# Attention and two feed-forward layers on one core: the last phase's weights brought to float32 during phase 1, their sums and splits spread over two steps, the gating product moved from GpSimd to VectorE

## The chip, the cores and the metric

The kernel runs on one core of a Trainium2 chip. The metric is device microseconds (us) of one execution; the median of the executions shown counts, and lower is better. Engines are called PE (TensorE, matrix multiply; PEld are its weight loads), DVE (VectorE), ACT (ScalarE), POOL (GpSimd) and SP (SyncE, which here only issues DMAs).

## The reference, cut to what matters

```python
x = attn(q, k, v, mem_k, mem_v)          # 3072 tokens x 512, chunked attention with 8 memory keys
h = x @ w_in                             # 512 -> 2048
x1 = softplus(h) @ w_out                 # 2048 -> 512
a, b = x1 @ w_a, x1 @ w_b                # 512 -> 1536 each
out = (a * b) @ w_o2                     # 1536 -> 512, float32
```

Inputs come as 64-bit floats, so every weight tile of 128 x 512 values (512 KB) is first brought to float32 by integer operations, and then split into a rounded high part and a low part; each product of two float32 matrices is made of three matmuls (high by high, high by low, low by high).

## The kernel before

The 3072 tokens are 8 tiles of 384. **Phase 1** runs, for each tile t and each of 16 f-steps, 12 matmuls of `emit_h` (L450), softplus and a split in `emit_soft` (L456 to L460, L437, L440), and, two f-steps later, 12 matmuls of `emit_x1` (L473), which accumulate x1; x1 goes to a scratch in DRAM (L481, L482). In tiles 0 to 6 the attention of later tokens is woven in by a list `plan` of (slot, step): tile t, f-step f stands at slots 2*(16*t+f) and the one after. In tile 0 the 32 tiles of w_in and w_out are converted and stay in SBUF, in the pool `wp` of 33 buffers with tag "w".

**The last phase** works on pairs of tiles (4 pairs p) in 12 steps f (`pair_step`). Of 2 x 2 blocks of x1 and of the weights w_a and w_b, sums are formed so that 7 products of 6 matmuls each (L623) do the work of 8 (a Strassen-Winograd scheme). The products run in the order X(11), Y(s2), W(s3), V(s1), X(12), W(22), V(s4); behind Y the DVE adds q = Y + s (L675), behind W r = W + q (L686), behind V d22 (L693); the second W product adds to the bank that r was read from, so it waits for r. c2 = d21 * d22 is formed on POOL (L703), rounded on ACT (L705), and its low part is formed on POOL (L706); c1 is formed on DVE (L714, ACT L716, DVE L717, the last one put off to the next step behind q). Between products, `next_job` runs parts of the output product (`job`, L646, six matmuls, then an addition on DVE, L655), six jobs for every two steps.

The weights of the last phase go through `Conversion`, one for each f: three fetches of 512 KB (w_a, w_b, w_o2; L548), an ACT operation on each (`top`, L532), two DVE operations on each (`val`, L534 and L535), four subtractions of 256 columns on POOL (`sums`, L566 to L569), the high parts on ACT (L579, L587), the low parts on POOL (L583) and DVE (L591), and five stores to scratches for pairs 1 to 3 (L598, L599). Conversions 0 to 2 run in tile 7 of phase 1, conversions 3 to 11 in pair 0, each within one step, three steps ahead of its use: `at(k)` is called seven times in a step, and runs the next entry of `steps()`. The sums and splits of x1 for pair 0 (`pieces`, L500 to L522) run on DVE in f-steps 10 to 15 of tile 7.

In tile 0, tile 7 and the last phase, the order of every engine's queue is the order of the program text; in tiles 1 to 6 that holds for PE and DVE alone, and a scheduler orders SP, ACT and POOL.

Of the kernel before, what the change touches and what calls it, by code (L numbers as in the profile page):

```python
# [9 lines left out]
F32 = mybir.dt.float32  # L10
# [7 lines left out]
TT = 384  # L18
# [18 lines left out]
LAST_CV = ((0, 4), (3, 7), (6, 10))  # L37
LAST_X1 = (7, 10)
PAIR_CV = 3
# [4 lines left out]
def attn_moe_moe2(ctx: ExitStack, tc: tile.TileContext, q, k, v, mem_k, mem_v,  # L44
# [28 lines left out]
    ud = nc.dram_tensor("u_scratch", (NF2, 4, P, 1024), F32, kind="Internal").ap()  # L73
    w2od = nc.dram_tensor("w2o_scratch", (NF2, P, 1024), F32, kind="Internal").ap()
# [413 lines left out]
    PLACE = {"11": (0, 0), "12": (0, 1), "s2": (1, 0), "s3": (1, 1), "s1": (2, 0), "22": (2, 1), "s4": (3, 0)}  # L488
# [35 lines left out]
    cv, us, w2o = {}, {}, {}  # L524

    def bits(val, raw, half):

        words = raw.rearrange("p (n two) -> p two n", two=2)
        low, high = words[:, 0], words[:, 1]
        if half == 0:  # L530
            top = high.bitcast(F32)
            nc.scalar.activation(top, top, AF.Prelu, scale=2.0 ** -112, alpha=-(2.0 ** 32))  # L532
        else:
            nc.vector.tensor_scalar(val, low, 29, None, ALU.logical_shift_right)  # L534
            nc.vector.scalar_tensor_tensor(val, high, 3, val, ALU.logical_shift_left, ALU.bitwise_or)  # L535

    class Conversion:


        def __init__(self, f):  # L540
            self.f = f
            self.raw = {}

        def fetch(self, n):
            f = self.f
            src = w_o2[f * P:(f + 1) * P, :] if n == "o" else (w_a if n == "a" else w_b)[:, f * P:(f + 1) * P].rearrange("(k p) f -> p k f", p=P)
            raw = self.raw[n] = wp.tile([P, 1024], U32, tag="w", name=f"raw_{n}{f}")
            nc.sync.dma_start(raw if n == "o" else raw.rearrange("p (a b) -> p a b", a=KT), src.bitcast(U32))  # L548

        def top(self, n):  # L550
            bits(None, self.raw[n], 0)

        def val(self, n):
            f = self.f
            if n == "a":
                self.v = wp.tile([P, 2, 512], U32, tag="w", name=f"v{f}")
            if n == "o":
                self.vo = mp.tile([P, 512], U32, tag="tmp", name=f"vo{f}", bufs=2)
            bits(self.vo if n == "o" else self.v[:, n == "b"], self.raw[n], 1)

        def sums(self, engine):
            v = self.v.bitcast(F32).rearrange("p n (k f) -> p n k f", k=2)
            b11, b21, b12, b22 = v[:, 0, 0], v[:, 0, 1], v[:, 1, 0], v[:, 1, 1]
            self.t = t = wp.tile([P, 4, 256], F32, tag="w", name=f"t{self.f}")
            t2, t3, t1, t4 = (t[:, i] for i in range(4))
            engine.tensor_tensor(t1, b12, b11, ALU.subtract)  # L566
            engine.tensor_tensor(t2, b22, t1, ALU.subtract)
            engine.tensor_tensor(t3, b22, b12, ALU.subtract)
            engine.tensor_tensor(t4, b21, t2, ALU.subtract)  # L569
# [94 lines left out]
    def pair_step(p, f, at, between=()):  # L664
# [11 lines left out]
        if late_lo:  # L676
            late_lo.pop()()
# [231 lines left out]
```

## Time and profile before

| what | value |
|---|---|
| median of 3 executions | 1280.59 us (1280.18 to 1280.63) |
| the profiled execution: its own time, its span | 1282.68 us, 1280.6 us |
| busy: PE, PEld, DVE, ACT, POOL | 94%, 88%, 54%, 42%, 30% of the span |
| tiles 1 to 6 of phase 1 | 154.7 to 604.3 us, 75 us each |
| tile 7 | 604.3 to 673.5 us |
| pair 0 | 673.5 to 855.05 us, 181.55 us |
| pairs 1 and 2 | 137.51 us each |
| pair 3 and the end | 1130.08 to 1280.6 us |

A stage ends where the first matmul of the next one starts. PE's matmuls are pipelined: six matmuls of 384 columns start 1.04 us apart as a group and six of 512 columns 1.39 us, so a step of a pair in which PE never waits takes 7 x 1.04 + 3 x 1.39 = 11.46 us; all steps of pairs 1 and 2 take that.

### The profile page before, as it was taken

The numbers are of one execution on the slowest core, as the hardware profiler recorded it, in microseconds if no ns is written. First come the engines' busy times: TensorE is split into PE (matmuls) and PEld (weight loads), VectorE is DVE, ScalarE is ACT, GpSimd is POOL, SyncE is SP. The second block draws the span as 40 slices with busy tenths as digits, with TensorE's granted clock in tenths as the row PEclk, the third lists the DMA queues.
The fourth block names the chain that finished last, engine by engine and source line by source line (L and its number), as shares of the span: only waits on it lengthen the run. The fifth ranks groups of instructions, "written<-read, shape, count | busy, mean of one in ns | idle before, by whom it ended". The sixth has DMA issues, their size and how long they took to land. (4 is left out here: it accounts for less than half of the span.)

```text
span 1280.6 us, 20711 instructions
## 1 busy us (share of the span) xinstructions
PE 1198.8 (94%) x7584; PEld 1124.7 (88%) x7584; DVE 692.4 (54%) x1618; ACT 540.4 (42%) x1333; POOL 383.0 (30%) x357
## 2 busy tenths in 40 slices
PE   5778899999999999999997888799999999999998
PEld 4677899999999999999996777699999999999997
DVE  4785644544444454444487666654445445553554
ACT  4775765565556555555663433222112111122110
POOL 1000023223222322222235776821144112431111
PEclk9997999999999999999998999899999999999999
DMA  8792313213041311300557777439844785549621
GB/s 177 200 292 56 68 37 57 55 30 71 12 75 37 58 48 31 73 14 13 188 215 252 269 251 275 180 129 329 298 170 148 249 342 192 204 150 383 211 87 50
DMA packets 205889, 191.30 MB, mean 149 GB/s; under 512 B 141659, under 2 KB 166363, under 8 KB 205787
## 3 DMA queue, kind: packets, MB, share of 16 engines
q1 hardware_dynamic: 205275, 189.90, 46.9%
q8 instruction: 60, 0.98, 0.3%
q14 instruction: 42, 0.34, 0.1%
q0 software_dynamic: 512, 0.07, 0.0%
HBM read 149.03 MB, written 40.89 MB: 148 GB/s over the span
## 5 line engine op out<-in xcount | busy, mean ns | idle before, releaser
L450 PE MATMUL ph<-x,w 128*128 128x384 f32 x1536 | 298.8, 342 | 12.8 <-ACT x L407 6.2
L450 PEld LDWEIGHTS ph<-x,w 128*128 128x128 f32 x1536 | 272.9, 192 | 18.9 <-ACT x L407 7.3
L646 PE MATMUL py<-w2o,c 128*128 128x512 f32 x864 | 227.3, 398 | 2.9 <-ACT c L705 1.8
L460 DVE SCALAR_TENSOR_TENSOR g<-ph,e 128x384 f32<-128x384 f32 x128 | 71.3, 557 | 266.8 <-ACT e L458 263.1
L646 PEld LDWEIGHTS py<-w2o,c 128*128 128x128 f32 x864 | 162.3, 190 | 31.7 <-POOL c L706 2.9
L705 ACT CAST c<-c 128x384 fp32r<-128x384 f32 x48 | 24.7, 514 | 328.6 <-POOL c L703 325.4
L703 POOL TENSOR_TENSOR c<-d,d 128x384 f32<-128x384 f32 x48 | 50.9, 1059 | 286.2 <-DVE d L701 286.2
L456 ACT ACTIVATE e<-ph 128x384 f32<-128x384 f32 x128 | 62.3, 487 | 136.0 <-PE ph L450 121.2
L623 PE MATMUL pX<-x,u 128*128 128x384 f32 x576 | 116.9, 337 | 2.6 <-ACT s L670 1.6
L655 DVE TENSOR_TENSOR y<-py,y 128x512 f32<-128x512 f32 x120 | 82.8, 690 | 61.7 <-PE py L646 61.7
L623 PEld LDWEIGHTS pX<-x,u 128*128 128x128 f32 x576 | 103.0, 190 | 7.8 <-ACT s L670 2.5
L623 PE MATMUL pW<-xx,u 128*128 128x384 f32 x288 | 63.0, 356 | 21.4 <-DVE r L686 21.4
L375 DVE STREAM_TRANSPOSE af<-sm 32x256 f32<-32x256 f32 x180 | 78.2, 435 | 2.5
L623 PEld LDWEIGHTS pW<-xx,u 128*128 128x128 f32 x288 | 53.7, 200 | 24.3 <-DVE r L686 24.3
L458 ACT ACTIVATE e<-e 128x384 f32<-128x384 f32 x128 | 67.3, 526 | 4.1
L457 ACT ACTIVATE e<-e 128x384 f32<-128x384 f32 x128 | 67.3, 526 | 4.0
L314 ACT ACTIVATE sm<-sm,st 128x96 f32<-128x96 f32 x168 | 60.6, 362 | 6.3 <-DVE st L310 6.3
L701 DVE TENSOR_TENSOR d<-pW,q 128x384 f32<-128x384 f32 x48 | 26.7, 557 | 66.8 <-PE pW L623 66.8
L623 PE MATMUL pV<-xs,u 128*128 128x384 f32 x288 | 58.7, 339 | 3.1 <-DVE xo L481 3.1
L623 PE MATMUL pV<-xx,u 128*128 128x384 f32 x288 | 59.1, 340 | 0.0
L623 PE MATMUL pW<-xs,u 128*128 128x384 f32 x288 | 57.9, 335 | 0.0
L623 PE MATMUL pY<-xs,u 128*128 128x384 f32 x288 | 57.6, 334 | 0.0
(232 smaller groups left out, 2234.7 us busy)
## 6 DMA issues: line engine op xcount, KB each, us to landing
u<-u_scratch SPq DMA_DIRECT2D x108, 512.0 KB
u_scratch<-u SPq DMA_DIRECT2D x36, 512.0 KB
w2o<-w2o_scratch SPq DMA_DIRECT2D x36, 512.0 KB
u<-u_scratch SPq DMA_DIRECT2D x36, 256.0 KB
raw<-in_moe_w_in_dram SPq DMA_DIRECT2D x16, 512.0 KB
raw<-in_moe_w_out_dram SPq DMA_DIRECT2D x16, 512.0 KB
vn<-in_v_dram SPq DMA_DIRECT2D x35, 176.0 KB
raw_a<-in_moe_w_a_dram SPq DMA_DIRECT2D x12, 512.0 KB
```

What stands on the lines that cost most here:

```text
L314: nc.scalar.activation(sm[:, h], sm[:, h], AF.Exp, bias=st[:, 0, h:h + 1], scale=-1.0, accum_out=st[:, 1, h:h + 1])
L375: nc.vector.transpose(out=af[32 * kb:32 * kb + 32, x], in_=self.sm[32 * x:32 * x + 32, :, 32 * kb:32 * kb + 32])
L450: nc.tensor.matmul(ph, lhsT=a, rhs=c, start=n == 0, stop=n == 3 * KT - 1)
L456: nc.scalar.activation(e, ph, AF.Abs)
L457: nc.scalar.activation(e, e, AF.Exp, scale=-1.0)
L458: nc.scalar.activation(e, e, AF.Ln, bias=1.0)
L460: nc.vector.scalar_tensor_tensor(g, ph, 0.0, e, ALU.max, ALU.add)
L623: nc.tensor.matmul(bank[:, :TT], lhsT=u[:, j, a, kt * P:kt * P + P], rhs=x[:, c, kt, :], start=first_ and m == 0, stop=m == 3 * KH - 1, sk ...
L646: nc.tensor.matmul(b, lhsT=c[:, x, r], rhs=w[:, y], start=n == 0, stop=n == 3 * GROUP - 1)
L655: tt(y, b, y, ALU.add)
L701: tt(d21, w[:, :TT], q, ALU.add)
L703: nc.gpsimd.tensor_tensor(c2, d21, d22, ALU.mult)
```

## The change

36 objects `Early` (12 f by w_a, w_b, w_o2) are put into `plan`, number n at slot 33 + 5.25 n: a fetch of the raw tile into the one spare buffer of `wp`, 3.2 slots later `top` on ACT, put behind the latest high-part copy of `emit_soft`; 5.2 slots later `value` (two operations on DVE); 6.2 slots later a store of the float32 values (256 KB) to a new scratch `vd`. They fall into tiles 1 to 6, and SP's queue is there now in the order of the program text too. `Conversion` now fetches the float32 values (512 KB for w_a and w_b, 256 KB for w_o2), forms the sums in three POOL operations in place of four, and is spread over 14 slots: conversions 0 and 1 run in tile 7, conversions 2 to 11 in pair 0, each over the second and the first step ahead of its use, with its stores one by one. The pieces of x1 for pair 0 start at f-step 8. In `pair_step`, c2 and its low part move from POOL to DVE; the low part stands behind c1.

```diff
-LAST_CV = ((0, 4), (3, 7), (6, 10))
-LAST_X1 = (7, 10)
-PAIR_CV = 3
+PRE_AT, PRE_BY = 33.0, 5.25
+PRE_STEPS = (0, 3.2, 5.2, 6.2)
...
+    vd = nc.dram_tensor("v_scratch", (NF2, 3, P, 512), U32, kind="Internal").ap()
...
-        nc.scalar.copy(hi, val)
+        anchor[0] = nc.scalar.copy(hi, val)
...
+    class Early:
...
+        def fetch(self):
+            f = self.f
+            self.raw = wp.tile([P, 1024], U32, tag="w", name=f"raw_{self.name}")
...
+        def top(self):
...
+            with tc.issue_after(anchor[0].ins):
+                nc.scalar.activation(top, top, AF.Prelu, scale=2.0 ** -112, alpha=-(2.0 ** 32))
+
+        def value(self):
+            self.val = val = mp.tile([P, 512], U32, tag="tmp", name=f"val_{self.name}", bufs=2)
+            nc.vector.tensor_scalar(val, self.low, 29, None, ALU.logical_shift_right)
+            nc.vector.scalar_tensor_tensor(val, self.high, 3, val, ALU.logical_shift_left, ALU.bitwise_or)
+
+        def store(self):
+            nc.sync.dma_start(vd[self.f, self.i], self.val)
...
+        def fetch(self):
+            self.v = wp.tile([P, 2, 512], F32, tag="w", name=f"v{self.f}")
+            nc.sync.dma_start(self.v.bitcast(U32), vd[self.f, 0:2].rearrange("n p f -> p n f"))
...
+        def add(self, i, engine=nc.gpsimd):
...
+                engine.tensor_tensor(self.t[:, 1:3], b[:, 2:4], v[:, :, 0:256], ALU.subtract)
+            elif i == 1:
+                engine.tensor_tensor(self.t[:, 0], v[:, 1, 256:], self.t[:, 1], ALU.subtract)
+            else:
+                engine.tensor_tensor(self.t[:, 3], v[:, 0, 256:], self.t[:, 0], ALU.subtract)
...
+        def slots(self):
+
+            c = self
+            return [lambda: c.add(0), lambda: (c.hi(0), c.add(1)), lambda: (c.hi(3), c.add(2)), lambda: c.lo(0),
+                    lambda: (c.hi(1), c.lo(3)), lambda: c.hi(2), lambda: c.store(0), lambda: c.lo(1),
+                    lambda: (c.lo(2), c.store(3)), lambda: None, lambda: c.store(1), lambda: None,
+                    lambda: c.store(2), lambda: None]
...
-        if late_lo:
-            late_lo.pop()()
+        while late_lo:
+            late_lo.pop(0)()
...
-        nc.gpsimd.tensor_tensor(c2, d21, d22, ALU.mult)
-        cs[p, f, 1] = c = wp.tile([P, 2, TT], F32R, tag="w", name=f"c{p}_{f}_1")
-        nc.scalar.copy(c[:, 0], c2)
-        nc.gpsimd.tensor_tensor(c[:, 1], c2, c[:, 0].bitcast(F32), ALU.subtract)
+        tt(c2, d21, d22, ALU.mult)
+        cs[p, f, 1] = cc = wp.tile([P, 2, TT], F32R, tag="w", name=f"c{p}_{f}_1")
+        nc.scalar.copy(cc[:, 0], c2)
...
+        tt(cc[:, 1], c2, cc[:, 0].bitcast(F32), ALU.subtract)
         late_lo.append(lambda: tt(c[:, 1], c1, c[:, 0].bitcast(F32), ALU.subtract))
...
+        for n in range(3 * NF2):
+            e = Early(*divmod(n, 3))
+            for d, step in zip(PRE_STEPS, (e.fetch, e.top, e.value, e.store)):
+                plan.append((PRE_AT + PRE_BY * n + d, 100 + n, step))
...
+        for a, f in ((4, 0), (12, 1)):
+            plan2.setdefault(a - 4, []).append(cvs[f].fetch)
+            for k, step in enumerate(cvs[f].slots()):
+                plan2.setdefault(a + k, []).append(step)
+        plan2.setdefault(10, []).append(partial(load_pair, 0))
...
-                early.enter_context(tc.manual_schedule(engines={engines["P"], engines["V"]}))
+                early.enter_context(tc.manual_schedule(engines={mybir.EngineType.SP, engines["P"], engines["V"]}))
...
+                        for g, kk in ((f + 1, 7 + k), (f + 2, k)):
+                            if 1 < g < NF2:
+                                cvs[g].slots()[kk]()
+                        if k == 3 and f + 3 < NF2:
+                            cvs[f + 3].fetch()
+                        if k == 1:
+                            cvs[f].hi_o()
+                        if k == 4:
+                            cvs[f].lo_o()
+                            if f + 1 < NF2:
+                                cvs[f + 1].fetch_o()
+                        if k == 1 and f > 0:
+                            cvs[f - 1].store_o()
```

## Rows read from the trace of the kernel before

**Rows 1.** By stage: busy us (instructions) of each engine, granted clock, DMA share, GB/s.

```profile
154.70:229.60 74.90, 73.96 (x576) 71.58 (x576) 35.28 (x116) 43.23 (x120) 21.07 (x21) 1.00 0.21 43
...
604.30:673.50 69.20, 67.56 (x384) 66.48 (x384) 43.72 (x65) 40.45 (x81) 22.34 (x21) 1.00 0.55 186
673.50:855.05 181.55, 150.17 (x709) 134.08 (x710) 124.41 (x187) 66.11 (x127) 120.03 (x108) 0.92 0.65 232
855.05:992.56 137.51, 137.51 (x721) 128.01 (x721) 68.84 (x117) 25.66 (x49) 40.66 (x33) 1.00 0.64 230
...
1130.08:1280.60 150.52, 146.28 (x757) 134.44 (x756) 72.22 (x123) 21.25 (x44) 25.42 (x26) 1.00 0.51 187
```

**Rows 2.** Waits of PE, 673 to 856 us: total us, times, longest.

```profile
PE pW L623 <- DVE r L686: 21.4, 9, 4.3
PE pV L623 <- DVE xo L481: 3.1, 1, 3.1
```

**Rows 3.** Timeline of pair 0: start, us, instruction, idle before it and releaser.

```profile
750.66 0.38 SPq L548 DMA_DIRECT2D raw_a<-in_moe_w_a_dram  x1
...
752.91 1.01 POOL L703 TENSOR_TENSOR c<-d,d 128x384 f32<-128x384 f32 x1
...
753.95 0.51 ACT L705 CAST c<-c 128x384 fp32r<-128x384 f32 x1 [4.91 <-POOL c L703]
...
756.48 1.59 DVE L591 TENSOR_TENSOR w2o<-vo,w2o 128x512 fp32r<-128x512 f32 x1 [3.72 <-ACT w2o L587]
756.72 0.67 ACT L532 ACTIVATE raw_a<-raw_a 128x512 f32<-128x512 f32 x1
...
758.46 1.16 DVE L717 TENSOR_TENSOR c<-c,c 128x384 fp32r<-128x384 f32 x1
...
761.27 0.55 DVE L686 TENSOR_TENSOR r<-pW,q 128x384 f32<-128x384 f32 x1
...
761.88 2.26 PE L623 MATMUL pW<-xx,u 128*128 128x384 f32 x6 [3.25 <-DVE r L686]
```

**Rows 4.** Timeline of a step of pair 1.

```profile
891.77 0.56 DVE L675 TENSOR_TENSOR q<-pY,s 128x384 f32<-128x384 f32 x1 [1.00 <-ACT s L670]
...
892.25 0.55 DVE L717 TENSOR_TENSOR c<-c,c 128x384 fp32r<-128x384 f32 x1
...
894.19 0.56 DVE L686 TENSOR_TENSOR r<-pW,q 128x384 f32<-128x384 f32 x1 [1.40 <-PE pW L623]
...
897.41 1.20 PE L623 MATMUL pW<-xx,u 128*128 128x384 f32 x6
```

**Rows 5.** Groups by line and shape, 604.3 to 855.05 us: count, busy us, mean ns, idle before.

```profile
L583 POOL TENSOR_TENSOR u<-t,u 128x512 fp32r<-128x512 f32 x24 | 36.5, 1542 | 0.0
...
L703 POOL TENSOR_TENSOR c<-d,d 128x384 f32<-128x384 f32 x12 | 12.9, 1078 | 13.6 <-DVE d L701 13.6
...
L535 DVE SCALAR_TENSOR_TENSOR v<-raw_b,v 128x512 uint32<-128x512 uint32 x12 | 8.3, 693 | 1.0
...
L532 ACT ACTIVATE raw_a<-raw_a 128x512 f32<-128x512 f32 x12 | 8.1, 674 | 0.0
...
L534 DVE TENSOR_SCALAR v<-raw_b 128x512 uint32<-128x512 uint32 x12 | 5.0, 418 | 0.0
```

**Rows 6.** Two lines' instructions, 604 to 855 us: ns least/median/most, first and last start.

```profile
L717 DVE TENSOR_TENSOR c<-c,c x11: 548/1168/1187, 700.4 to 846.4; 128x384 fp32r<-128x384 f32 x11
...
L591 DVE TENSOR_TENSOR w2o<-vo,w2o x12: 675/1470/1593, 639.3 to 822.9; 128x512 fp32r<-128x512 f32 x12
```

**Rows 7.** Timeline of tiles 2 and 4: tightest hand-over to PE, and a store's wait.

```profile
270.62 1.02 POOL L440 TENSOR_TENSOR g_7l<-g,g_7h 128x384 fp32r<-128x384 f32 x1
...
273.33 0.33 PE L473 MATMUL px<-g_7l,w 128*128 128x384 f32 x1
...
393.29 0.49 ACT L456 ACTIVATE e<-ph 128x384 f32<-128x384 f32 x1 [1.94 <-DMA x_scratch<-xo]
```

**Rows 8.** Timeline at the end of pair 3.

```profile
1268.71 3.94 PEld L646 LDWEIGHTS py<-w2o,c 128*128 128x128 f32 x18 [0.22 <-POOL c L706]
```

More of the change, by code (lines that the diff above doesn't have):

```diff
@@ L432, in attn_moe_moe2 @@
     acc = {}
+    anchor = [None]
     def split(val, name, engine=nc.gpsimd, between=None):
@@ L522, in split_lo, with __init__ @@
         engine.tensor_tensor(x[:, 1], raws[n], x[:, 0].bitcast(F32), ALU.subtract)
[L524 to L535, printed above, removed]
+    us, w2o = {}, {}
+    class Early:
+        def __init__(self, f, i):
+            self.f, self.i = f, i
+            self.name = f"{'abo'[i]}{f}"
+        def fetch(self):
+            f = self.f
+            self.raw = wp.tile([P, 1024], U32, tag="w", name=f"raw_{self.name}")
+            if self.i == 2:
+                nc.sync.dma_start(self.raw, w_o2[f * P:(f + 1) * P, :].bitcast(U32))
+            else:
+                src = (w_a, w_b)[self.i][:, f * P:(f + 1) * P].rearrange("(k p) f -> p k f", p=P)
+                nc.sync.dma_start(self.raw.rearrange("p (a b) -> p a b", a=KT), src.bitcast(U32))
+        def top(self):
+            words = self.raw.rearrange("p (n two) -> p two n", two=2)
+            self.low, self.high = words[:, 0], words[:, 1]
+            top = self.high.bitcast(F32)
+            with tc.issue_after(anchor[0].ins):
[6 more added lines that the diff above has]
+            nc.sync.dma_start(vd[self.f, self.i], self.val)
     class Conversion:
@@ L541, in __init__ @@
             self.f = f
[L542 to L569, printed above, removed]
+        def fetch(self):
+            self.v = wp.tile([P, 2, 512], F32, tag="w", name=f"v{self.f}")
+            nc.sync.dma_start(self.v.bitcast(U32), vd[self.f, 0:2].rearrange("n p f -> p n f"))
@@ new lines, in fetch_o @@
+        def fetch_o(self):
+            self.vo = mp.tile([P, 512], F32, tag="tmp", name=f"vo{self.f}", bufs=2)
+            nc.sync.dma_start(self.vo.bitcast(U32), vd[self.f, 2])
+        def add(self, i, engine=nc.gpsimd):
+            v = self.v
+            if i == 0:
+                self.t = wp.tile([P, 4, 256], F32, tag="w", name=f"t{self.f}")
+                b = v.rearrange("p n (k f) -> p (n k) f", k=2)
+                engine.tensor_tensor(self.t[:, 1:3], b[:, 2:4], v[:, :, 0:256], ALU.subtract)
+            elif i == 1:
+                engine.tensor_tensor(self.t[:, 0], v[:, 1, 256:], self.t[:, 1], ALU.subtract)
+            else:
+                engine.tensor_tensor(self.t[:, 3], v[:, 0, 256:], self.t[:, 0], ALU.subtract)
@@ L809, in order @@
                 else:
-                    for what in plan2.pop(f, ()):
-                        what()
-                    emit_soft(t, f, ph, nc.vector, slot, slot)
-                    if f >= LAST_X1[1]:
-                        for _ in range(-(-len(pieces) // (NF1 - f))):
-                            pieces.pop(0)()
+                    emit_soft(t, f, ph, nc.vector, partial(slot, 2 * f), partial(slot, 2 * f + 1))
                 att_at(2 * (NF1 * t + f))
@@ L822, in between_0 @@
             emit_x1(*pend.pop(0))
-        while todo:
-            todo.pop(0)()
-        for s in sorted(plan2):
-            for what in plan2[s]:
-                what()
-        n_fetched = [0]
+        assert not plan2
         for p in range(NTILE // 2):
@@ L856, in at @@
                             fetch_o(*nxt)
+                    if p == 1 and (f, k) == (0, 1):
+                        cvs[NF2 - 1].store_o()
                     if more:
```

75 lines of the change are left out of this document (26 added, 49 removed).

## The prediction, made before the changed kernel ran

> **What bounds the kernel now.** I read the busy time by stage first [rows 1]. In tiles 1 to 6, and in pairs 1 to 3, PE is busy 97 to 100% of the time; nothing on another engine matters there as long as it stays hidden. Pair 0 is the exception: it takes 181.55 us where pair 1 takes 137.51, and DVE (124.41 us), POOL (120.03) and PE (150.17) are all partly idle, which says that they wait for each other. What would pair 0 take if PE never waited? Pair 1's 137.51, less six jobs that only come later (pair 0 runs 30 of 36; 6 x 1.39 = 8.3), plus the last two x1 steps of tile 7, which run inside it (24 matmuls, 4 x 1.04 = 4.2): 133.4 us. So 48.2 us are lost there. PE is idle for 31.4 of them (181.55 - 150.17); most of the rest is clock, since the granted clock is 0.92 there against 1.00 elsewhere (8% of 181.55 = 14.5 us) [rows 1]. It falls where PE stands, so it should come back with the stalls.
>
> The waits say whom PE waits for: nine times the second W product waits for r on DVE, 21.4 us in all, longest 4.3 [rows 2]. The timeline of one step shows why r is late [rows 3], followed backward: r ends at 761.82 and PE, 3.25 us idle, starts at 761.88. DVE is late because it stood 3.72 us before the low part of w2o, waiting for ACT, and then did two operations of a conversion's value. ACT was late because its copy of c2 stood 4.91 us for POOL's c2. And c2, one operation of 1.01 us, is queued on POOL behind the sums and splits of the conversion. It is a ring through four queues, each in program order. In a step of pair 1 the same r starts 894.19, still waiting 1.40 us for PE itself, and the W product that needs it starts at 897.41: 2.7 us of room [rows 4].
>
> **The change part by part.**
>
> *Pair 0.* (a) c2 and its low part leave POOL, so ACT's copy of c2 no longer waits behind conversions. (b) The six value operations leave DVE: by the w_b rows (0.418 + 0.693) three tiles cost 3.3 us a step; three ACT operations of 0.674 leave too, 2.0 us [rows 5]. (c) The copy of w2o stands at k=1, its low part at k=4 behind the fifth product, so DVE reaches it some 6 us after ACT. All links of the ring are cut.
>
> What DVE gains is c2 and a low part. I take 0.55 us each, the cost of the same form without POOL beside it [rows 4]; beside POOL's conversions that form takes up to 1.19, and the low part of w2o up to 1.59 instead of 0.68 [rows 6]. DVE's sum per step: pair 1's 68.84 / 12 = 5.74 [rows 1], plus 2 x 0.55 + 0.68 = 7.5 us; with all four two-input operations beside POOL, 5.74 + 0.64 + 2 x 1.19 + 1.59 = 10.35 us. Both are under 11.46. For r, the new low part of c2 lands ahead of q, where DVE now waits 1.00 us for ACT [rows 4]: 0.55 disappears in it, 1.19 shows 0.2. The low part of c1 behind q adds up to 0.64. Together 0.84, against r's 1.40 of waiting and 2.7 of room. So no stall in the ordinary step.
>
> POOL: 120.03 us in pair 0 [rows 1], less c2 and its split (12 x 1.08 and about the same again, 25 us [rows 5]), plus one conversion (ten instead of nine: four low parts and the sums, some 9 us): 104 of 137 us. It has slack of 2.7 us a step, and its results are used a full step later. Step 8 adds four sums of pair 1's x1 to its queue, a backlog of most of a step that ends two steps later; the ACT copies that wait for it have half a step: 0 to 1 us.
>
> The buffers: before, up to four conversions' parts lie in the 33 buffers, and by my count of the program text 31 to 37 are wanted from step 2 to step 9, so fetches and copies wait for PE. After, the count is 12 to 24 up to step 6 and at most 30. I charge nothing for buffers.
>
> The start keeps some loss. V of step 0 waits for DVE's first copy of x1 (0.6 us and hand-over, now 3.1 [rows 2]): 1 us. In step 0, SP's fetch of v for conversion 3 is queued behind four x1 stores that wait for those copies; step 1 has no jobs and is only 7.3 us long, so ACT's first copy of conversion 3 may hold ACT's queue (s and c of step 2 behind it): 0 to 6 us, I take 2. With 0.5 for step 8, pair 0 becomes 133.4 + 3.5 = 136.9: a gain of 44.7, bounds 36 and 48.
>
> *Tile 7.* It loses the nine value and ACT operations of conversions, and the pieces end four slots earlier. It takes 69.20 us, of which 66.7 is PE's floor (384 matmuls at 0.1735) [rows 1]. Gain 1, bounds 0 and 2.
>
> *Tiles 1 to 6.* 36 times 0.674 on ACT and 1.11 on DVE [rows 5], that is 4 and 7 us a tile, on engines busy 43.23 and 35.28 of 74.90 [rows 1]. The tightest hand-over I found is a low part that POOL finishes at 271.64 and PE takes at 273.33 [rows 7]: 1.7 us of room, so one operation in the way (1.11, or 0.67) hides; both together (1.8) would show 0.1. The fetch has 3.2 slots, 7.5 us; a fetch of the same form was issued at 750.66 with two more behind it, and ACT used it at 756.72 without waiting [rows 3], so 6.1 us is an upper bound. SP's queue becomes program order: a fetch now waits there for the value before it, with attention's loads and the x1 stores queued behind. Each such wait is on work that stands earlier in the program, so it costs at most a transfer ahead of an x1 store. ACT already waits 1.94 us for such a store [rows 7], with PE unaffected. Loss 2 us in all, bounds 0 and 8.
>
> *Pairs 1 to 3 and the end.* DVE's 5.74 a step becomes 6.84, PE keeps 11.46; nothing. But at the very end no products stand between c2's low part and the first job: POOL's low part is 0.22 us late already [rows 8], and behind d12 and c1 on DVE it comes about 0.8 later. Loss 0.8.
>
> **A rule against it.** The rows show DVE's two-input operation going from 0.55 to 1.19 at most beside POOL [rows 6]: it shares. The Trainium skill, page "SBUF — State Buffer", section "Who interferes with whom", says that VectorE with two SBUF inputs and a reading GpSimd contend for a port pair as an exclusive lock, the second blocking until the first is done. By that rule a gating product on VectorE would wait for a whole GpSimd operation; rival 2 gives its price, and the eleven rows, none over 1.19, speak against it.
>
> **The sum.** The profiled execution took 1282.68 us, its span 1280.6, 2.08 lying around it. 1282.68 - 44.7 - 1 + 2 + 0.8 = 1239.8. The median, 1280.59, is 2.1 below the profiled time, so I forecast 1238 us. Own range: from all gains and no losses, 1230.5, to 36 gained, 8 and 0.8 lost, 1253.
>
> **The rivals.**
>
> 1. *Forecast*, the ring is cut and PE bounds pair 0: 1238 us, chance 0.74.
>
> 2. *DVE becomes the bound of pair 0.* If each two-input operation waits for a whole POOL operation (mean 1.54 for a split [rows 5]), DVE needs 5.74 + 1.54 + 2 x 2.09 + 2.23 = 13.7 us a step, 2.2 over PE's 11.46, in ten steps 22 us: 1260. For it: four such operations a step where there were two. Against: 1.19 and 1.59 as the most seen [rows 6]. The same size would come from ACT waiting 2 us a step for a fetch of v behind the stores; DMA is at 0.65 of its time and would go to about 0.74. Chance 0.17.
>
> 3. *Slower: ACT held in tiles 1 to 6.* Were the raw tile to land late, ACT would stand at `top`, with softplus of the next f-steps behind it, and DVE at `value`. The gain of 42 us is eaten at 42 / 36 = 1.2 us of PE time for each conversion; with 1.7 us of room, ACT must be held 2.9 us, a landing over 10.4 us after the fetch's issue. At 12.4 us (3.2 lost each) the time is 1238 + 36 x 3.2 = 1353 less what the wider hand-overs absorb, about 1310. For it: small packets of attention's loads share the queue. Against: 6.1 us above, and a DMA share of 0.21 [rows 1]. Chance 0.05.
>
> 4. *It doesn't do what it says:* SP, in order, sticks behind stores that wait for POOL, conversions come late, and pair 0 keeps its time: 1280. For it: SP is one queue for fetches and stores alike. Against: the stores are now one by one, each a slot or more after its split. Chance 0.04.
>
> **How the numbers follow.** 0.2% (2.6 us) is about what a measurement tells from no change. Faster: rivals 1 and 2 and a third of 4, 0.92; same, 0.03; slower, 0.05. The range, leaving the tails out and reaching into rival 2: 1230 to 1257.
>
> **What would show it.** Right: pair 0 of 134 to 142 us, clock 1.00 there, no wait of W for r over 1 us, steps 3 to 9 at 11.46, ACT's copy of c2 waiting for DVE under a microsecond beyond d21; tiles of 75 to 76 us; a PE wait of about 1 us before the last jobs. Wrong: two-input DVE operations of 2 us and steps of 13 us (rival 2); ACT idle on a raw tile's DMA and tiles over 76.5 us (rival 3); pair 0 above 160 us with POOL or SP waits (rival 4).

## The result and the profile after

The changed kernel takes **1261.68 us** (median of 4, 1260.66 to 1264.58) where the kernel before took 1280.38 in the same comparison: ratio 0.9858, 95% interval 0.9841 to 0.9876. It is faster by 1.4%, the way that was forecast, but by 18.7 us and not by the 42.6 forecast: the time lies 4.7 us above the upper end of the range.

The busy time by stage, of after (columns as in [rows 1]: the stretch, its length, busy time and instructions of PE, PEld, DVE, ACT and POOL, granted clock, DMA share, GB/s). The second to seventh lines are tiles 1 to 6 one by one:

```profile
0.00:150.10 150.10, 109.66 (x840) 97.98 (x840) 103.01 (x315) 99.08 (x260) 7.58 (x22) 0.87 0.68 169
150.10:231.00 80.90, 76.70 (x577) 73.74 (x577) 40.75 (x127) 46.87 (x127) 22.04 (x21) 0.96 0.38 93
231.00:310.80 79.80, 75.47 (x577) 72.95 (x577) 42.08 (x130) 46.64 (x129) 23.71 (x23) 0.97 0.43 104
310.80:394.40 83.60, 76.98 (x576) 73.92 (x576) 41.55 (x129) 46.47 (x129) 21.65 (x19) 0.95 0.42 99
394.40:475.50 81.10, 76.11 (x577) 73.16 (x577) 42.05 (x130) 46.98 (x129) 21.74 (x19) 0.96 0.41 100
475.50:552.30 76.80, 76.11 (x576) 73.51 (x576) 41.11 (x125) 46.32 (x126) 21.74 (x19) 0.97 0.39 96
552.30:631.60 79.30, 75.42 (x577) 72.96 (x577) 44.87 (x131) 47.95 (x128) 21.83 (x20) 0.98 0.34 96
631.60:698.96 67.36, 67.08 (x385) 66.64 (x386) 36.73 (x54) 35.88 (x71) 20.94 (x18) 1.00 0.35 122
698.96:832.49 133.53, 133.53 (x709) 125.33 (x709) 98.06 (x149) 50.78 (x101) 92.69 (x75) 1.00 0.77 285
...
1107.53:1258.50 150.97, 146.45 (x757) 134.44 (x756) 85.18 (x149) 20.71 (x43) 0.00 (x0) 1.00 0.51 187
```

Against the stages of before [rows 1], one profiled execution against the other (their spans differ by 22.1 us, the medians by 18.7):

| stage | before, us | after, us | difference | the prediction's term |
|---|---|---|---|---|
| start and tile 0 | 154.7 | 150.1 | -4.6 | none |
| tiles 1 to 6 | 449.6 | 481.4 | **+31.8** | +2 (0 to +8) |
| tile 7 | 69.2 | 67.4 | -1.8 | -1 |
| pair 0 | 181.5 | 133.5 | -48.0 | -44.7 (-36 to -48) |
| pairs 1 and 2 | 275.0 | 275.0 | 0 | 0 |
| pair 3 and the end | 150.5 | 151.0 | +0.5 | +0.8 |

Pair 0 sits at its floor: PE is busy for all of its 133.53 us, at a granted clock of 1.00. Tiles 1 to 6 gave most of it back. PE does the same work there, but each tile takes 76.8 to 83.6 us in place of 75, and the clock is 0.95 to 0.98 where it was 1.00. From the starts of the f-steps in both traces, f-step 15 of tiles 1 to 4 grew by 16 us in sum, f-step 0 of the six tiles by 14. The waits of that stretch say who holds PE (engine, line, what it waited for: us in all, times, longest), the first line in the kernel before, the others after:

```profile
PE ph L450 <- ACT x L407: 5.5, 6, 2.0
...
PE ph L451 <- ACT x L407: 22.5, 7, 5.7
ACT raw_o L548 <- DMA raw_o<-in_moe_w_out_dram: 16.0, 6, 4.2
ACT raw_b L548 <- DMA raw_b<-in_moe_w_b_dram: 12.7, 8, 3.7
PE ph L451 <- DVE x L408: 3.5, 2, 3.2
DVE kt L341 <- DMA kn<-in_k_dram: 2.9, 1, 2.9
```

PE's first product of a tile waits for ACT's copy of the last block of x, 26 us in all with DVE's part; the kernel before has 5.5 for ACT's. And ACT waits about as long, 28.7 us, for raw tiles of the last phase's weights. The timeline of one tile's end shows how the two hang together:

```profile
215.29 0.41 SPq L541 DMA_DIRECT2D raw_b<-in_moe_w_b_dram  x1
...
222.54 0.69 DVE L553 SCALAR_TENSOR_TENSOR val_b<-raw_b,val_b 128x512 uint32<-128x512 uint32 x1
...
224.72 0.47 SPq L172 DMA_DIRECT2D qn<-in_q_dram  x1
225.30 0.40 SPq L538 DMA_DIRECT2D raw_o<-in_moe_w_out_dram  x1
...
226.01 1.15 PE L400 MATMUL pxa<-af,vn 96*64 96x64 f32 x32
...
229.81 0.65 ACT L548 ACTIVATE raw_o<-raw_o 128x512 f32<-128x512 f32 x1 [2.97 <-DMA raw_o<-in_moe_w_out_dram]
230.37 0.57 ACT L407 CAST x<-pxa 128x512 fp32r<-128x512 f32 x1
...
230.99 0.44 PE L451 MATMUL ph<-x,w 128*128 128x384 f32 x1 [3.83 <-ACT x L407]
```

SP issued 36 loads of k and q between 203.6 and 225.2, 0.47 us for most of them, with one raw fetch among them at 215.29; only then, at 225.30, the fetch of the raw tile that ACT waits for. `top` could use it 4.5 us later. `top` stands on ACT ahead of the x copy, whose input `pxa` was complete at 227.2; the copy came at 230.37, and PE's next tile at 230.99. So the raw tile was not slow, it was asked for late. Two things make it late, one behind the other. All raw tiles go through one spare buffer, which was free again when DVE had read the tile before, at 223.23: from there the fetch stood 2.1 us behind loads. And the tile before was late itself: its buffer was free at 209.69, and its fetch, among the loads, was issued at 215.29.

The loads are hurt in turn. At the end of tile 5, DVE's transposes of k (`kt`), which stand ahead of DVE's part of x, waited 2.9 us for k, and PE 3.2 us for that part of x (both among the longest waits of the rows above); f-step 0 of tile 6 took 10.0 us in place of 5.7.

### The profile page after: what moved, and what is told of

The parts are those of the page before. It is cut to its first block, busy times and chain, and to the rows that moved or that the text cites. A ratio compares the mean times of both kernels' runs of the same rounds, so it can differ in the third digit from the quotient of the medians.

```text
span 1258.5 us, 20769 instructions
## 1 busy us (share of the span) xinstructions
PE 1188.6 (94%) x7584; PEld 1120.7 (89%) x7584; DVE 739.5 (59%) x1714; ACT 539.0 (43%) x1333; POOL 285.2 (23%) x249
## 4 chain that ended last, share of the span: by engine, by line
PE 79%; SPq 6%; ACT 4%; DVE 4%; DMA 4%; issue 1%; DVEq 0%
PE ph L451 17%; PE py L661 16%; PE px L474 16%; PE pV L638 8%; PE pX L638 8%; PE pW L638 8%; PE pY L638 4%; SPq L172 2%; SPq L170 2%; PE sc L357 2%; DMA raw_o<-in_moe_w_out_dram 1%; PE pxa L400 1%; DVE af L375 1%; ACT sm L314 1%; SPq L252 1%
## 5 line engine op out<-in xcount | busy, mean ns | idle before, releaser
L451 PE MATMUL ph<-x,w 128*128 128x384 f32 x1536 | 307.6, 349 | 30.9 <-ACT x L407 22.5
L451 PEld LDWEIGHTS ph<-x,w 128*128 128x128 f32 x1536 | 280.7, 197 | 37.6 <-ACT x L407 23.7
L661 PE MATMUL py<-w2o,c 128*128 128x512 f32 x864 | 223.2, 394 | 0.7 <-DVE c L731 0.5
L720 ACT CAST c<-c 128x384 fp32r<-128x384 f32 x48 | 24.7, 515 | 304.0 <-DVE c L718 271.4
L730 ACT CAST c<-c 128x384 fp32r<-128x384 f32 x48 | 24.6, 514 | 77.8 <-DVE c L728 76.8
L638 PE MATMUL pW<-xx,u 128*128 128x384 f32 x288 | 57.6, 334 | 0.0
L638 PEld LDWEIGHTS pV<-xx,u 128*128 128x128 f32 x288 | 51.5, 188 | 4.2
```

The source lines that it names most:

```text
L451: nc.tensor.matmul(ph, lhsT=a, rhs=c, start=n == 0, stop=n == 3 * KT - 1)
L638: nc.tensor.matmul(bank[:, :TT], lhsT=u[:, j, a, kt * P:kt * P + P], rhs=x[:, c, kt, :], start=first_ and m == 0, stop=m == 3 * KH - 1, sk ...
L661: nc.tensor.matmul(b, lhsT=c[:, x, r], rhs=w[:, y], start=n == 0, stop=n == 3 * GROUP - 1)
```

## The experiments

### The gating alone, on the kernel before

```diff
-        nc.gpsimd.tensor_tensor(c2, d21, d22, ALU.mult)
+        tt(c2, d21, d22, ALU.mult)
...
-        nc.gpsimd.tensor_tensor(c[:, 1], c2, c[:, 0].bitcast(F32), ALU.subtract)
...
+        tt(cc[:, 1], c2, cc[:, 0].bitcast(F32), ALU.subtract)
```

> The kernel before with one part of the change alone: c2 and its low part on DVE. Theory (a ring of queues, of which c2 on POOL is one link): ACT's copy of c2 no longer waits for POOL (66 us of waits in pair 0 before), but the value operations, ACT's copies behind POOL's sums and the low part of w2o stay, so pair 0 falls from 181.5 to between 150 and 170 us, the whole to 1248 to 1270. Rival (the conversion's work in pair 0 is what counts, not where c2 stands): pair 0 stays above 175, the whole above 1274. Tiles 1 to 6 stay at 449.6 in both.

Measured: 1264.05 us, ratio 0.9875 (0.9858 to 0.9892), as the theory expected. Pair 0 took 163.4 us (181.5 before), tiles 1 to 6 449.7, as before.

### The changed kernel with the gating left on GpSimd

```diff
-        tt(c2, d21, d22, ALU.mult)
+        nc.gpsimd.tensor_tensor(c2, d21, d22, ALU.mult)
...
+        nc.gpsimd.tensor_tensor(cc[:, 1], c2, cc[:, 0].bitcast(F32), ALU.subtract)
...
-        tt(cc[:, 1], c2, cc[:, 0].bitcast(F32), ALU.subtract)
```

> The changed kernel with c2 and its low part back on POOL, everything else as changed. Theory (the ring through POOL, ACT and DVE was what pair 0 lost its time to, and c2's place in POOL's queue is a link of it that must be cut): POOL then has some 11 us of work in a step of 11.46, ACT's copy of c2 waits for it again, and pair 0 takes 140 to 155 us instead of 133.5. Rival (taking the conversion's first half and the buffers' load out of pair 0 is enough): pair 0 takes 133.5 to 136. Pairs 1 to 3 stay at 137.5 in both.

Measured: 1272.56 us in a single run; pair 0 took 145.75, inside the theory's 140 to 155. The waits in pair 0 of this kernel:

```profile
ACT c L720 <- POOL c L718: 60.5, 11, 10.7
DVE q L690 <- ACT s L685: 25.8, 11, 6.5
```

ACT still stands up to 10.7 us for POOL's c2, and DVE's q behind it. That does not lengthen every step: steps 2, 9 and 10 (counted from 0) take 15.7, 13.7 and 17.4 us, all others from step 3 on 11.46; in steps 9 and 10 c2 is queued behind the sums and splits of pair 1's x1. So of pair 0's 48.0 us the gating alone gives 18.1, all other parts without it 35.8, and both 48.0: each cuts part of the same ring, and the floor takes the rest. The prediction's account of pair 0 holds.

### The changed kernel without its fetches

```diff
+            if Early.one is not None:
+                self.raw = Early.one
+                return
-            self.raw = wp.tile([P, 1024], U32, tag="w", name=f"raw_{self.name}")
+            self.raw = Early.one = wp.tile([P, 1024], U32, tag="w", name=f"raw_{self.name}")
```

> The changed kernel without 35 of the 36 raw fetches: all conversions work on the first raw tile, in the same slots, with the same ACT and DVE operations and the same stores (the last phase's weights are therefore not the reference's). Theory (the late fetch is the cause): tiles 1 to 6 take 450 to 458 us, the whole some 1230 to 1236. Rival (the added operations are the cause): tiles 1 to 6 stay above 475, the whole above 1252.

Measured: 1233.19 us, a single run. The kernel leaves out 35 of the 36 fetches; the operations, the stores and the order of SP's queue stay. Its tiles 1 to 6, by the same view as above:

```profile
151.97:604.09 452.12, 444.88 (x3456) 429.10 (x3456) 251.86 (x768) 280.94 (x760) 132.66 (x120) 1.00 0.27 64
```

452.1 against 449.6 before: the 36 operations of ACT, the 72 of DVE, the 36 stores and SP's order cost 2.5 us together, which is the prediction's term of 2. The other 29 us come with the fetches.

### The fetches on GpSimd's queue

```diff
-                nc.sync.dma_start(self.raw, w_o2[f * P:(f + 1) * P, :].bitcast(U32))
+                nc.gpsimd.dma_start(self.raw, w_o2[f * P:(f + 1) * P, :].bitcast(U32))
...
-                nc.sync.dma_start(self.raw.rearrange("p (a b) -> p a b", a=KT), src.bitcast(U32))
+                nc.gpsimd.dma_start(self.raw.rearrange("p (a b) -> p a b", a=KT), src.bitcast(U32))
```

> The changed kernel with the 36 raw fetches issued from POOL's queue instead of SP's, in the same slots; everything else as changed. If SP's issue queue is what makes them late (some 0.5 us for each of 40 loads ahead), they are issued as soon as the buffer is free, ACT's waits for raw tiles at the tiles' ends go from 3 to 4 us to under 1, attention's loads no longer stand behind a fetch that waits for DVE, and tiles 1 to 6 take 452 to 465 us, the whole 1232 to 1246. If the DMA engines' backlog is what counts, the tiles stay at 472 or more, the whole above 1252.

Measured: 1248.58 us, ratio 0.9763 (0.9746 to 0.9779), between the two expectations; tiles 1 to 6 took 468.4. The stall has moved: f-step 15 is back at 6.1 to 7.4 us, and f-step 0 of tiles 2, 3 and 5 takes 8.6 to 11.2 us in place of 6. The loads of k and q are the ones that now come late. From SP's queue of this kernel, the issues over 1 us between 206 and 230 (the first is four loads in one row):

```profile
206.54 2.07 SPq L183 DMA_DIRECT2D kn<-in_k_dram  x4
...
212.57 2.51 SPq L172 DMA_DIRECT2D qn<-in_q_dram  x1
...
216.66 1.58 SPq L172 DMA_DIRECT2D qn<-in_q_dram  x1
```

The usual issue is 0.47 us, and the kernel before has one of 1.3 to 1.8 us in each of tiles 1 to 5 too; here there are two, and the one of 2.51 came while a fetch that POOL had issued at 209.58 was under way. The last of the 36 was out at 226.1, and DVE, which had waited 3.49 us, began the transposes of k (kt) at 228.86, 2.8 us later. (The profile puts the end of that wait down to a store that SP had issued right behind the loads, at 226.18; kt itself reads k.)

### The same, with an eighth of the bytes

```diff
+            if Early.one is not None:
+                self.raw = Early.one
+                if self.i == 2:
+                    nc.gpsimd.dma_start(self.raw[:, 0:P], w_o2[f * P:(f + 1) * P, 0:P // 2].bitcast(U32))
+                else:
+                    nc.gpsimd.dma_start(self.raw[:, 0:P], (w_a, w_b)[self.i][0:P, f * P:f * P + P // 2].bitcast(U32))
+                return
```

> As the kernel that only moves the fetches to GpSimd (1248.6 us), but each fetch after the first brings 64 KB in place of 512 KB, into a raw tile shared by all chains; the last phase's weights are therefore not the right ones, all other work stands. If the fetches hurt the loads of k and q by the DMA engines' time, the 17 us that are left above the run without fetches shrink to 5 or less: 1231 to 1238 us. If it is the chain (the wait of GpSimd for the raw tile, the order of the operations on ScalarE) and not the bytes, it stays at 1244 to 1250 us.

Measured: 1238.39 us, tiles 1 to 6 457.4. The kernel leaves out seven eighths of the bytes of 35 fetches. Of the 16.3 us that the fetches on POOL cost above no fetches (468.4 - 452.1), 11 go with the bytes; 5.3 stay. At the end of tile 1 the last load was out at 225.3 and kt began 1.6 us later (226.92), where it was 2.8 us with all the bytes. It is a single run, as is the one without fetches, and the expectation's bound (1238) is missed by 0.4.

### SP's order left to the scheduler

```diff
-                early.enter_context(tc.manual_schedule(engines={mybir.EngineType.SP, engines["P"], engines["V"]}))
+                early.enter_context(tc.manual_schedule(engines={engines["P"], engines["V"]}))
```

> The changed kernel with one part undone: in tiles 1 to 6 SP's queue is ordered by the scheduler again, as before the change. The raw fetches still stand among attention's loads there. Theory (what counts is that a fetch stands behind some 30 loads, not who ordered the queue): tiles 1 to 6 stay at 472 to 490 us, the whole within 8 us of 1262. Rival (the order of the program text on SP delays attention's loads and the stores of x1): tiles 1 to 6 return to 450 to 458, the whole to 1230 to 1238.

Measured: 1252.27 us, ratio 0.9772 (0.9753 to 0.9792); tiles 1 to 6 took 471.1. Neither expectation was met: the theory's lower bound is missed by 1 us in the tiles and by 2 us in the whole, the rival's 450 to 458 by 13. So 10 us hang on SP's order in the text, and 19 above no fetches remain: order alone was not the cause.

### Six chains in the front of each tile

A chain is the four steps of one `Early` (fetch, `top`, `value`, store); a slot is half an f-step.

```diff
-PRE_AT, PRE_BY = 33.0, 5.25
-PRE_STEPS = (0, 3.2, 5.2, 6.2)
+PRE_AT, PRE_BY = 33.0, 3.8
+PRE_STEPS = (0, 2.8, 3.75, 3.78)
...
-                plan.append((PRE_AT + PRE_BY * n + d, 100 + n, step))
+                plan.append((PRE_AT + 2 * NF1 * (n // 6) + PRE_BY * (n % 6) + d, 100 + n, step))
```

> The changed kernel with the 36 early conversions moved inside their tiles: six in each of tiles 1 to 6, 3.8 slots apart, the sixth fetched just ahead of attention's loads and none after slot 24 of a tile, so that no raw fetch stands on SP's queue behind the 32 loads of k and q and no raw tile is awaited on ACT ahead of the copy of x that the next tile starts with. Theory (the fetch is issued late behind those loads, and ACT stands at the raw tile with x's copy behind it): tiles 1 to 6 fall from 481 us to 450 to 458, the granted clock there returns to 1.00, the whole to 1230 to 1238 us. Rival (the 36 times 0.67 us on ACT and 1.11 us on DVE are in the way themselves, wherever they stand): the denser spacing makes tiles 1 to 6 no better, 475 us or more, the whole 1255 to 1270.

Measured: 1265.46 us, ratio 0.9875 (0.9859 to 0.9892), tiles 1 to 6 483.9: the expectation of my theory at that time fell. The numbers are those of the rival, but the kernel without fetches, with all of the rival's operations, excludes its reason. f-step 15 is back at 6.1 or 6.2 us, and f-step 0 of tiles 2 to 6 takes 11.5 to 12.6 us. SP and then DVE at the end of tile 1 of this kernel:

```profile
207.34 0.33 SPq L556 DMA_DIRECT2D v_scratch<-val_b  x1
207.76 0.38 SPq L538 DMA_DIRECT2D raw_o<-in_moe_w_out_dram  x1
208.20 0.44 SPq L170 DMA_DIRECT2D kn<-in_k_dram  x1
```

```profile
230.69 0.71 DVE L341 STREAM_TRANSPOSE kt<-kn 128x512 f32<-128x512 f32 x1 [4.34 <-DMA kn<-in_k_dram]
```

This is the second half of the cause. The loads of k and q began at 208.2, 55.8 us after the tile's start, because a store and a fetch in front of them waited for DVE's value; in the kernel before they began at 205.9, 51.2 us after it, and had ended their issue 3.0 us before DVE's kt. What is 4.6 us late in the queue has become 6.1 us in f-step 0 of tile 2 (11.9 for 5.8). The same stands at the end of tiles 2 to 5, where kt waits 3.3 to 5.0 us.

The same with 3.1 slots between the chains and steps at 0, 2.3, 3.05 and 3.08:

> The changed kernel with the 36 early conversions packed into the part of each tile in which SP issues no loads of k and q: six in each of tiles 1 to 6, 3.1 slots apart from slot 1, the last value at slot 19.6, ahead of the loads that begin at 20.2; ACT's operation 2.3 slots behind the fetch. Theory (SP's queue and the DMA rings are full from slot 20 to the tile's end, and both the raw tile and the next tile's k and q are late when a fetch stands among them): no wait for a raw tile ahead of x's copy and none of DVE for k, tiles 1 to 6 at 452 to 462 us against 481, the whole 1232 to 1243 us. Rival (the denser operations, or transfers of 512 KB anywhere in a tile, cost as much): 470 us or more, the whole 1252 or more.

Measured: 1272.45 us, ratio 0.9938 (0.9921 to 0.9954), tiles 1 to 6 491.4: worse than the change as it is, and again in the rival's range. A chain needs 4.2 us of landing, 0.67 on ACT and 1.1 on DVE, and its successor's fetch waits for the one spare buffer; at 3.1 slots (some 7 us) `top` waits for 25 of the 36 raw tiles, and the waits stand in the middle of a tile too. Three of the waits of this kernel in tiles 1 to 6:

```profile
ACT raw_b L548 <- DMA raw_b<-in_moe_w_b_dram: 18.7, 11, 3.5
...
PE pxa L400 <- DVE af L375: 17.0, 6, 3.0
...
PE ph L451 <- DVE x L408: 8.1, 7, 3.9
```

`af` is formed for the block of x in the middle of a tile, and f-step 10 became 8.5 to 10.9 us (f-step 0 of tiles 5 and 6 9.6 and 11.8). So a tile has two tight points, its middle and its end, where an attention unit is handed over.

### Chains kept away from both points

```diff
+PRE_TILES = ((6, 3.4), (5, 3.9), (6, 3.4), (5, 3.9), (5, 3.9), (9, 3.4))
+PRE_AT = [32 * (t + 1) + 0.3 + by * i for t, (n, by) in enumerate(PRE_TILES) for i in range(n)]
+PRE_STEPS = (0, 2.5, 3.3, 3.35)
...
-                plan.append((PRE_AT + PRE_BY * n + d, 100 + n, step))
+                plan.append((PRE_AT[n] + d, 100 + n, step))
```

> The 36 chains stand in the first 21 half-steps of tiles 1 to 5 (6, 5, 6, 5, 5 of them, 3.4 or 3.9 half-steps apart; one half-step is about 2.34 us) and 9 in tile 6, which has no loads of k and q to make. Still all on SyncE's queue. Theory A: what costs the time is that SyncE's 36 loads of k and q (0.5 us each, about 20 us, from 51 us after a tile's start on) share queue and DMA engines with the chains' fetches and stores, at a point where they have no slack, and that a raw tile which is fetched behind them is late. Then the loads start at 51 us again in each tile, kt waits for nothing, f-step 15 and f-step 0 are back at about 6 us, tiles 1 to 6 last 452 to 458 us (the run without fetches 452) and the kernel 1233 to 1241 us. Theory B: the 36 fetches of 512 KB cost their 29 us wherever they stand, for instance by taking bandwidth from the x1 stores or by chains that are late in themselves. Then tiles 1 to 6 stay at 468 us or more and the kernel at 1249 us or more.

Measured: 1262.9 us, ratio 0.9857 (0.9836 to 0.9878): by the times alone, theory B. But the stretch falls in two: tiles 1 to 4 took 306.8 us (without fetches 302.0), tiles 5 and 6 together 171.8. In tiles 4 and 5 the last store stood ahead of the loads, which began 55 and 62 us after the tile's start (7 of the 62 are the longer f-step 0 of tile 5 itself), and f-step 0 of tiles 5 and 6 took 12.6 and 11.7 us. Tile 6, with nine chains, lost another 6 us in f-step 10.

The same places with the fetches on GpSimd:

> The same places for the chains, with the fetches issued by GpSimd. Theory A: the queue no longer matters once the stretch of the k and q loads is free of fetches: within 3 us of the kernel with the same places on SyncE, 1232 to 1243 us. Theory B: the fetches cost what they do in the kernel that only moves them to GpSimd, 1246 to 1251 us. If it is slower than the one on SyncE by over 4 us, GpSimd's own work, the lo halves of g, waits behind the fetch for the raw tile to come free.

Measured: 1269.53 us, ratio 0.9897 (0.9872 to 0.9922), slower than on SP by 6.6: POOL waited 29.5 us, in 17 waits, for a raw tile to come free, and the low parts of g and the softmax of attention are queued behind those waits.

The next version puts each tile's last store behind the loads, and gives the chains more room:

```diff
+PRE_TILES = ((6, 3.5), (5, 3.9), (6, 3.5), (5, 3.9), (6, 3.5), (8, 3.85))
+PRE = [(32 * (t + 1) + 0.3 + by * i, by, 30.0 - by * i if t < 5 and i == n - 1 else 0)
+       for t, (n, by) in enumerate(PRE_TILES) for i in range(n)]
...
+            at, by, last = PRE[n]
+            for d, step in ((0, e.fetch), (by - 0.9, e.top), (by - 0.15, e.value), (last or by - 0.1, e.store)):
+                plan.append((at + d, 100 + n, step))
```

> As the kernel with 6, 5, 6, 5, 5 and 9 chains in tiles 1 to 6, with two edits: in tiles 1 to 5 the last chain's store stands at half-step 30, behind the 36 loads of k and q on SyncE, so that nothing on that queue waits for VectorE in front of the loads; and the chains have more room, 3.5 half-steps where a tile holds 6 (tiles 1, 3, 5), 3.9 and 3.85 where it holds 5 or 8 (tile 6). Theory A (the loads must start by 53 us after a tile's start and be issued without a gap; in the kernel with 6, 5, 6, 5, 5, 9 they began at 55 us in tiles 4 and 5 behind a store, and f-step 0 of tiles 5 and 6 became 12 us): the loads start at 51 to 53 us in every tile, f-step 0 is 5.7 to 6.3 us in every tile, tiles 1 to 6 take 454 to 464 us, the kernel 1235 to 1246 us. Theory B (the loads are late for another reason, such as the fetches' use of the DMA engines earlier in the tile): f-step 0 stays at 9 us or more in at least two tiles and the kernel at 1250 us or more.

Measured: 1247.85 us, ratio 0.9748 (0.9728 to 0.9767), again between the two. Its tiles 1 to 4 and 5 to 6:

```profile
151.47:454.26 302.79, 297.12 (x2304) 286.16 (x2304) 168.28 (x507) 185.27 (x504) 86.65 (x82) 1.00 0.42 102
454.26:616.13 161.87, 151.79 (x1153) 146.35 (x1153) 87.12 (x259) 95.22 (x256) 42.93 (x39) 0.97 0.38 102
```

The first line speaks for theory A: 22 chains with all their bytes, all on SP, for 302.8 us against 302.0 in the kernel that fetches nothing. What went wrong at the end of tile 4 began in its middle:

```profile
429.40 0.66 ACT L549 ACTIVATE raw_a<-raw_a 128x512 f32<-128x512 f32 x1 [1.27 <-DMA raw_a<-in_moe_w_a_dram]
429.96 0.51 ACT L460 ACTIVATE e<-e 128x384 f32<-128x384 f32 x1
```

```profile
425.33 0.39 SPq L542 DMA_DIRECT2D raw_a<-in_moe_w_a_dram  x1
432.11 0.33 SPq L171 DMA_DIRECT2D kn<-in_k_dram  x1
```

ACT stood 1.27 us for a raw tile just ahead of softplus of the f-step in which DVE transposes the previous k (431.05); that sets k's buffer free, and SP, whose queue had been empty since 425.7, could start the loads at 432.11 only, 53.1 us after the tile's start. 1.9 us late there became 3.8 us in f-step 0 of tile 5. Most of the rest of these two tiles' loss lies in f-step 10 of tile 5 (8.5 us for 5.5) and f-step 15 of tile 6 (10.0 for 6.1).

The last version has 3.5 half-steps in every tile (`PRE_TILES, PRE_BY = (6, 5, 6, 5, 6, 8), 3.5`):

> As the kernel with 6, 5, 6, 5, 6 and 8 chains and the late last stores (1247.9 us; its tiles 1 to 4 took 75.3 to 76.7 us, as without fetches, but tiles 5, 6 and 7 together 18 us more), with 3.5 half-steps between the chains in every tile. There the raw tile's wait on ScalarE in tile 4 stood at half-step 18.9, 1.27 us in front of the x copy and the transposes of the middle of the tile, which set the buffers of k and q free, and the loads of tile 4 began 53.1 us after its start in place of 51.1. Theory A (the middle and the end of a tile are the two points without slack; elsewhere a chain costs next to nothing): with the last wait at half-step 16.9 in tile 4, and at 27.4 in tile 6, f-step 0 of tile 5 is back at 6 us, f-step 15 of tile 6 at 6.1 us, tiles 1 to 6 take 453 to 460 us and the kernel 1234 to 1242 us. Theory B (the fetches cost some 15 us in sum wherever they stand, and tiles 1 to 4 were the lucky half): tiles 1 to 6 stay at 468 us or more, the kernel at 1248 us or more.

Measured: **1243.08 us** (median of 5, 1240.41 to 1244.37), ratio 0.9711 (0.9698 to 0.9724), the fastest version that does all of the work; 1 us above the upper end of theory A, and clear of theory B. Tiles 1 to 6 and pair 0 of its profiled execution:

```profile
150.95:611.21 460.26, 447.80 (x3456) 431.23 (x3456) 257.29 (x768) 281.31 (x760) 131.93 (x120) 0.99 0.41 104
...
678.60:812.17 133.57, 133.57 (x709) 125.33 (x709) 98.27 (x149) 50.80 (x101) 92.69 (x75) 1.00 0.77 285
```

460.3 us are 21 less than in the change as it was made, and 8 more than without fetches; the profile is of the fastest of the five executions, and the medians of the two kernels differ by 18.6. ACT waits for raw tiles no less than it did (16.0, 12.7 and 1.5 us by tile in the change as it was made):

```profile
ACT raw_a L549 <- DMA raw_a<-in_moe_w_a_dram: 12.4, 8, 3.0
ACT raw_b L549 <- DMA raw_b<-in_moe_w_b_dram: 11.3, 7, 4.4
ACT raw_o L549 <- DMA raw_o<-in_moe_w_out_dram: 10.1, 6, 3.2
```

So it is the place of the waits that counts, not their sum. f-step 0 is at 5.8 or 5.9 us in tiles 2 to 6; some 5 of the 8 us are in f-step 10 of tiles 4 to 6 (7.0 to 7.3 us for 5.5), where `top` still waits for a raw tile up to 2.6 us shortly before the middle. Whether a second raw buffer would take that wait away is open: there is no room in SBUF for one.

## Why the prediction was wrong, step by step

**Pair 0** (forecast 136.9, bounds 133.5 to 145.5): right in mechanism, a little too careful in size. The ring is cut, every step from 3 to 11 takes 11.46 us, and the clock came back to 1.00. Of the 3.5 us charged for the start and step 8 nothing showed beyond 0.2. DVE's busy time is 98.06 / 12 = 8.2 us a step, inside the 7.5 to 10.35.

**Rival 2** (DVE becomes the bound) did not come, but the reading that spoke against it ("it shares", from 1.19 us at most) was wrong. The two-input operation for c2 of after; then one of the twelve, with the POOL operation that was under way; then two POOL operations of before, in a row, the second of which was under way when DVE's low part of c1 started at 758.46 [rows 3]:

```profile
L718 DVE TENSOR_TENSOR c<-d,d x12: 557/557/1512, 710.1 to 831.0; 128x384 f32<-128x384 f32 x12
...
738.97 1.29 POOL L578 TENSOR_TENSOR t<-v 128x512 f32<-128x512 f32 x1
739.17 1.51 DVE L718 TENSOR_TENSOR c<-d,d 128x384 f32<-128x384 f32 x1
...
756.22 2.98 POOL L583 TENSOR_TENSOR u<-t,u 128x512 fp32r<-128x512 f32 x2
```

Both DVE operations end 0.42 us after the POOL operation (740.68 after 740.26; 759.62 after 759.20). It is the same for every other one: of the twelve c2, seven ran while POOL stood idle and took 0.56 us each, and the other five ended 0.41 to 0.46 us after the POOL operation that they met; of the eleven in [rows 6], the nine that met one ended 0.41 or 0.42 us after it. DVE does not share here, it waits for the rest of POOL's operation. The Trainium skill's page "SBUF — State Buffer", section "Who interferes with whom", has a VectorE operation with two SBUF inputs and a GpSimd operation that reads SBUF contend for an exclusive lock, so that the second waits until the first is done; the trace agrees. Rival 2 did not come because a wait is for what is left of the POOL operation, not for a whole split (1.54 [rows 5]), and because seven of the twelve met none: the mean of c2 (0.82) stayed far under what would fill a step. That rival 2's price, 1260 us, is close to the 1261.68 measured is chance, since pair 0 is at its floor.

**Tile 7** and **the end**: -1.8 for -1, +0.5 for +0.8. **Start and tile 0**: -4.6, not forecast. No run here took that stage apart. Its text is the same in all of these kernels, the one before included, and tile 1 began between 150.9 and 153.7 in the others, so up to 3.6 us of it come and go without any edit; it is luck, not the change, as far as the runs tell.

**Tiles 1 to 6** is the step that failed: +31.8 for +2, bounds 0 to 8. Its first half was right: the operations cost 2.5 us, stores and SP's order included. Three of its sentences were wrong.

- *"The tightest hand-over I found ... 1.7 us of room."* I looked at low parts of g inside a tile [rows 7]. The tightest hand-over is at the end of a tile, where PE's first product waits for the copy of x in the kernel before already, 5.5 us in six waits. There is no room there: what ACT stands, PE stands.
- *"The fetch has 3.2 slots, 7.5 us"*, with 6.1 us as an upper bound for landing. Where ACT waited for it, the tile was there 3.9 to 4.7 us after its issue, once 6.0: inside the bound. But the slots count from the place in the text, and the issue came up to 12 us after PE had passed that place. The fetch first needs the spare buffer: 26 of the 35 later fetches went out within 0.4 us of the moment at which DVE had read the tile before. The nine that stand among the loads went out 2.1 to 9.1 us after it. A DMA's time starts when its queue gets to it and its buffer is free.
- *"Each such wait ... costs at most a transfer ahead of an x1 store."* The prediction names attention's loads behind these waits and puts no price on them. In the kernel before they take 19 of the 24 us between the middle of a tile and its end (205.9 to 225.0, with tile 2 from 229.6 on), and don't start earlier: k's buffer is set free by the transposes in the middle, and the first load goes out 1.06 us after these start (204.80 and 205.86 here, 202.58 and 203.64 in after). A wait of 2 us in front of them, or a fetch of 512 KB beside them, comes out at the next tile's start.

So the costs of the fetch came in two ways, and the runs tell them apart (tiles 1 to 6, one profiled execution each): taking the text's order from SP gives 10 us back, taking the fetches off SP 13, and an eighth of the bytes another 11; keeping all of it, but clear of the loads and of both hand-overs, gives 21.

**Rival 3** was this mechanism under another condition. It asked for a landing over 10.4 us and priced it at 1310; the landing never came near that (6.0 at most where ACT waited), and its signs were seen all the same: ACT idle on a raw tile's DMA, tiles over 76.5 us. Two fifths of its loss were enough to leave the range. Its condition should have been the time from the place in the text to landing, with the spare buffer and SP's queue in between, not the landing alone.

With 31.8 for this term and all others as forecast, the sum for the profiled execution would be 1269.6; 3.4 us more from pair 0, 4.6 from the start and 1.1 from tile 7 and the end bring it to 1260.5, and 1260.66 was measured.

## What to carry to other kernels

When DMAs are put into a queue, list what that queue issues in the stretch, with the time that each issue takes, and find the point at which the next wave of loads may start and the point at which it is needed: the slack is what lies between, less the issues and the last landing. Here DVE used k 3.0 us after the last issue had ended, in a tile of 75 us with a DMA share of 0.21 [rows 1]. Look for the tightest hand-over at the seams of the loops, where the trace of before shows the main engine waiting already, not in their middle. And give an operation on a fetched tile its place by when the queue can have issued the fetch; ahead of a critical operation on the same engine, a tile that comes late holds that operation too.

## What the runs showed of the hardware

A wait of 3.8 us on PE costs more than itself. Around the tile's end above (the wait ends at 230.99), the same view of after in short stretches:

```profile
228.00:230.00 2.00, 0.00 (x0) 0.00 (x0) 0.00 (x0) 0.18 (x1) 0.00 (x0) 1.00 0.95 322
...
231.00:232.00 1.00, 0.72 (x2) 0.46 (x3) 0.66 (x1) 0.17 (x2) 0.00 (x0) 0.66 0.18 40
232.00:233.00 1.00, 1.00 (x4) 1.00 (x5) 0.00 (x0) 0.00 (x0) 0.00 (x0) 0.50 0.00 0
233.00:234.00 1.00, 1.00 (x5) 1.00 (x4) 0.00 (x0) 0.00 (x0) 0.00 (x0) 0.50 0.00 0
234.00:236.00 2.00, 2.00 (x38) 1.65 (x36) 0.00 (x0) 0.66 (x2) 0.00 (x0) 0.82 0.00 0
236.00:240.00 4.00, 4.00 (x28) 3.98 (x24) 2.96 (x19) 3.28 (x14) 1.02 (x1) 1.00 0.02 4
```

The same end of a tile in the kernel before:

```profile
229.64:232.00 2.36, 2.08 (x10) 1.82 (x11) 0.67 (x1) 0.18 (x2) 0.08 (x1) 1.00 0.69 153
```

The granted clock, 1.00 before and in the wait, is 0.50 (1.2 GHz) from 232 to 234, in the work that follows, and 1.00 (2.4 GHz) again from 236 on: f-step 15 grew by 3.1 us, and f-step 0 behind it by another 1.4. In the kernel before, PE waits 0.7 us ahead of the first product and 0.3 just behind it, and the clock stays at 1.00.

And a DMA has a price on its issuing queue, which does not go by its bytes: 0.47 us for most loads of k and q (48 KB), 0.33 to 0.41 for most fetches of 512 KB, so that SP is busy with issuing loads for 17 to 19 us of each of tiles 1 to 5 of the kernel before. A row of busy engines doesn't show that, since DMA issues are not counted there.
